# Merging the two halves of float64 weights: the low word's bits made on ScalarE, one VectorE pass instead of two

## The chip, the cores and the metric

The kernel runs on one core of one Trainium2 chip. The core has five engines that work side by side and wait for each other through semaphores: TensorE (PE; its weight loads are listed as PEld), VectorE (DVE), ScalarE (ACT), GpSimd (POOL) and SyncE (SP), which here mostly issues transfers. The metric is the time of one execution on the device, in microseconds (us); the time of a kernel is the median of several runs.

## The reference

The computation is a recurrent attention (an mLSTM) over 768 steps, for 4 batches and 8 heads of width 40, followed by a feed-forward layer over 3072 tokens of width 320 with 2048 hidden units:

```
for t in range(S):
    m_new = max(f[t] + m, i[t]);  f_s = exp(f[t] + m - m_new);  i_s = exp(i[t] - m_new)
    C = f_s * C + i_s * outer(v[t], k[t]);   n = f_s * n + i_s * k[t]
    y[t] = sigmoid(o[t]) * (C @ q[t]) / max(abs(n @ q[t]), 1)
h = x @ w_in                       # x: y by token, (3072, 320) @ (320, 2048)
g = max(h, 0) + alpha * min(h, 0)
out = g @ w_out                    # (3072, 2048) @ (2048, 320)
```

The weights w_in and w_out arrive as float64. The kernel computes in float32, with each operand of the large products split into a high part (fp32r) and a low part (the rest).

## The kernel before, in words

**Attention.** The recurrence is computed in chunks of 128 tokens, 24 chunks in all, two of which make a group of 256 tokens. For a chunk, TensorE makes scores from k and q by channel (tiles kf and qf), ScalarE makes the decays E as exponentials (L909 in the first group, L425 behind it), GpSimd masks them, VectorE weighs the scores (L933, L447), and TensorE multiplies them with the values and adds the part of the carried state C. The gated result xn is transposed, split (XH, XL, X2, X2L) and handed to the feed-forward layer.

**Feed-forward.** For each group there are eight steps fp. `up` makes 256 hidden units of 256 tokens (L593 to L600, in PSUM tile ph). ScalarE's Relu (L602) and a VectorE pass (L606) apply the slopes; a ScalarE cast makes the high part gh (L614) and VectorE or GpSimd the low part gl (L615). `down` multiplies them with the high and low parts of w_out (OH, OL) into po (L623).

**Weights.** Class `Weights` converts one tile. There are 18 tiles: eight of w_in with 128x512 values (t_wi), two that hold the rest of w_in's rows (t_wr, 128x512), and eight of w_out with 128x640 values (t_wo). A tile's raw float64 values are seen as pairs of 32-bit words: `raw[..., 1]` is the high word and `raw[..., 0]` the low word, so each is read at every second word. The steps are

1. `scale` (L696), on ScalarE: the high word, read as a float, goes through Prelu with a scale and a slope chosen so that the exponent is brought to float32's range and the sign is kept, in tile t.
2. `join` (L708 and L710), on VectorE: the bits of t are shifted left by 3, and then the top three bits of the low word (shifted right by 29) are merged in.
3. `high` (L718), on ScalarE: the cast to the high part WH, OH or W2.
4. `low` (L722), on VectorE: t less the high part.

The raw tiles of w_in lie in room that later holds parts of w_out; those of w_out share two buffers, so SyncE's queue loads a further one only when the step `join` has read an earlier one (L762).

**Order.** The work of the first group is written out by hand in the string ORDER: every name is a step (`w0s` is the scale step of weight tile 0, `w1h` its high part for tile 1, `kc1` and `qc1` copies of k and q by channel, `L1` a scan on VectorE, `wg10` a weighing, `warm12` twelve dummy matmuls that keep TensorE busy), and the instructions of each engine are chained in this order. ORDER covers the scale, join and split of tiles 0, 1 and 2. What follows it, from about 33 us on, is issued in the order of the program and placed on each engine by a planner, which goes by its own estimates of durations: the last tiles of the first half of w_in (`for t in w[3:]: t.all()`), then `convert("in", ...)` and `convert("out", ...)` ahead of the feed-forward steps that need them, interleaved with steps of the attention (`side`). All weights stay in SBUF from then on; the later groups convert none.

The functions around the change, with the line numbers of the profile:

Of the kernel before, what the change touches and what calls it, by code (L numbers as in the profile page):

```python
# [10 lines left out]
U32 = mybir.dt.uint32  # L11
BF16 = mybir.dt.bfloat16
AF = mybir.ActivationFunctionType
ALU = mybir.AluOpType
# [3 lines left out]
def kernel(ctx: ExitStack, tc: tile.TileContext, q, k, v, i_gate, f_gate, o_gate, w_in, w_out, alpha, out):  # L18
    nc = tc.nc
# [46 lines left out]
    def staging(name, tag):  # L66
        t = const.tile([P, NB * DM], U32, tag=tag, name=name)
        return t[:, : 2 * CW].rearrange("p (c w) -> p c w", w=2)

# [54 lines left out]
    def open_gate(b, c0=0, c1=NC):  # L124
        og = o_tiles[b][:, c0:c1]
        nc.scalar.activation(og, og, AF.Sigmoid)
# [14 lines left out]
    def weighed(n):  # L141

        b, c = divmod(n, NC)
        kd = sb.tile([P, H, D], F32, tag="kd", name=f"kd{n}")
        (nc.gpsimd if n in KDP else nc.vector).tensor_tensor(
            kd, by_token_of(n, 1), wT[:, c, b * H : (b + 1) * H].unsqueeze(2).broadcast_to([P, H, D]), ALU.mult
        )
        kds[n] = kd
# [152 lines left out]
    def values(n, E, busy=lambda: None):  # L301

        pH = psa(f"pH{n}")
        dense(pH, FILL.get(n, 0))
        va = va_t[n // GC % NV][:, n % GC]
        for i in range(H):
            if i % 2 == 0:
                busy()
            par, p = divmod(i, NPR)
            h = 2 * p + par  # L310
            nc.tensor.matmul(
                pH[:, h * VA : (h + 1) * VA], E[par][:, p * P : (p + 1) * P], va[:, h], start=True, stop=True
            )
        return pH[:, : H * VA].rearrange("p (h e) -> p h e", e=VA)
# [205 lines left out]
    def attention(n0):  # L520
# [45 lines left out]
    FILL = {3: 4, 4: 14, 5: 4}  # L566
    ORDER = """dq0 dq1 dw0 dw2 warm24 dv0 dw1 dw4 do1 dw3 do2 scan lf0a lf0b li0 lf0z L0 bj0 qT0 qc0 kT0 kc0 warm12 sp00
        bTt bTc l3a l3b alT l3c l3d warm6 wt0 ex00 sc00 l3e ms00 warm3 sp01 ewj ex01 ms01 sc01 warm3 eeL wg00 wTt eTt
        wTc eTc lf1a lf1b warm3 w0s wg01 sp10 alC ex10 ms10 warm3 sp11 ex11 qT1 w1s kT1 kc1 w0j0 warm4 li1 wd0 w0j1 w2s
        warm12 u0m qc1 u0c v0 w0h w0l w1j0 L1 w2j0 warm2 sc10 w1j1 warm2 w2j1 wd1 wg10 fsm fst sc11 ms11 warm6 dv1 dq3 wg11 og1  # L570
        lpa lpb bj1 dq2 dL dx2 w1h g0r dx0 g0g lpc lpd lpe g0x g0p w1l dx1 v1 x0 warm4 tadd g1r g1g s0a w2h g1x g1p w2l warm12 x1
        s1a s1d warm3 s0d og2"""

# [102 lines left out]
    class Weights:  # L676
# [11 lines left out]
        def scale(self):  # L688
            shape = list(self.raw.shape[:-1])
            t = late_pool.tile([P, 2 * DM], F32, tag="t", name=f"t_{self.name}", bufs=3)  # L690
            if len(shape) == 3:
                self.t = t.rearrange("p (f c) -> p f c", c=shape[2])
            else:
                self.t = t[: shape[0], : shape[1]]
            if self.double:
                nc.scalar.activation(  # L696
                    self.t, self.raw[..., 1].bitcast(F32), AF.Prelu, scale=2.0**-112, alpha=-(2.0**32)
                )
            else:
                for rows, src, _, _ in self.pieces:  # L700
                    nc.sync.dma_start(self.t[rows], src)

        def join(self, steps=range(2)):
            if self.double:
                t, lo = self.t.bitcast(U32), self.raw[..., 0]
                for step in steps:
                    if step == 0:
                        nc.vector.tensor_scalar(t, t, 3, None, ALU.logical_shift_left)  # L708
                    else:
                        nc.vector.scalar_tensor_tensor(t, lo, 29, t, ALU.logical_shift_right, ALU.bitwise_or)  # L710

        def parts(self, piece):
            rows, _, h, l = self.pieces[piece]
# [19 lines left out]

    ROOM = [["OH1", "OL1", "OH2"], ["OL2", "OH3"], ["OL3", "OH2", "OL2"], ["OH3", "OL3"]]
    CW = 512

    def load_w_in(i, kt):

        c0 = i * CW
        half, h0 = divmod(c0, DH)  # L740

        def part(X):
            return lambda: X[half][:, kt, h0 : h0 + CW]

        src = w_in[kt * P : (kt + 1) * P, c0 : c0 + CW]
        return Weights(f"wi{i}_{kt}", staging(f"wi{i}_{kt}", ROOM[i][kt]), [(slice(0, P), src, part(WH), part(WL))])

    def load_w_rest(i):

        pieces = []  # L750
        for e in range(2):
            cs = slice((i + e) * CW, (i + e + 1) * CW)
            rows, other = (slice(x * KR, (x + 1) * KR) for x in (e, 1 - e))
# [57 lines left out]
    def first_group():  # L811
# [12 lines left out]
        f, i, rst, m = fi[:, 0, :S], fi[:, 1, :S], rm[:, 0, :S], rm[:, 1, : S + 1]  # L824
# [4 lines left out]
        w = [None] * 5  # L829
# [115 lines left out]
        def warm(n=1):  # L945
            dense(junk, n)
# [19 lines left out]
        steps = {}  # L966
# [8 lines left out]
        def first_lf(j, t, engine):  # L975
            engine.tensor_tensor(lf[j], f[:, t], m[:, t], ALU.add)

        def second_lf(j, u, engine):
            engine.tensor_tensor(lf[j], lf[j], m[:, u], ALU.subtract)
# [37 lines left out]
        def later_decays():  # L1017
# [21 lines left out]
            lf1a=lambda: first_lf(1, t1, nc.gpsimd), lf1b=lambda: second_lf(1, u1, nc.gpsimd),  # L1039
            li0=lambda: nc.gpsimd.tensor_tensor(li[:, t0], i[:, t0], m[:, u0], ALU.subtract),  # L1040
            li1=lambda: nc.gpsimd.tensor_tensor(li[:, t1], i[:, t1], m[:, u1], ALU.subtract),
# [6 lines left out]
            wd0=lambda: weighed(0), wd1=lambda: weighed(1),  # L1048
            v0=lambda: got.update(h0=values(0, [E[0, 0], E[0, 1]], lambda: warm(V0))),
            v1=lambda: got.update(h1=values(1, [E[1, 0], E[1, 1]], lambda: warm(V1))),  # L1050
            og1=lambda: open_gate(0, 0, GC), og2=lambda: open_gate(0, GC, NC),
# [32 lines left out]
        for j in range(3):  # L1084
            steps[f"w{j}s"] = lambda j=j: w[j].scale()
            steps[f"w{j}h"] = lambda j=j: w[j].high()
            steps[f"w{j}l"] = lambda j=j: w[j].low()
            for step in range(2):
                steps[f"w{j}j{step}"] = lambda j=j, step=step: w[j].join([step])
        for name in ORDER.split():  # L1090
            if name.startswith("warm"):
                warm(int(name[4:]))
# [29 lines left out]
    late_pool = ctx.enter_context(tc.tile_pool(name="late", bufs=2))  # L1122
    start = len(nc.cur_bb.bb.instructions)
    first = first_group()
    next(first)
    pinned = pin(start)
# [81 lines left out]
```

## Time and profile before

| | |
|---|---|
| median of 3 runs | 497.78 us (497.69 to 501.44) |
| span of the profiled execution | 497.0 us (its time as a run is not given apart from this) |
| TensorE busy | 479.6 us, 97% of the span |
| VectorE busy | 324.1 us, 65% |
| ScalarE busy | 321.4 us, 65% |
| GpSimd busy | 305.9 us, 62% |
| conversion of the weight tiles | from 14.5 us (first Prelu) to about 98 us (last low part) |

The profile is one execution on the chip. Its page gives busy times of the engines; further views give the instructions of a line or a tile, what an engine waited for, the chain of work that ended last, the engines' instructions in order of time, and busy times by stretch of the span. In a list in order of time, a row has the start and the duration in us, then engine, line, operation and tiles, and in brackets the idle time before it and what ended that. A matmul's neighbours overlap, so rows of TensorE add up to more than the time they take together; the same holds in part for two instructions in a row on VectorE or ScalarE.

### The profile page before, as it was taken

The numbers are of one execution on the slowest core, as the hardware profiler recorded it, in microseconds if no ns is written. First come the engines' busy times: TensorE is split into PE (matmuls) and PEld (weight loads), VectorE is DVE, ScalarE is ACT, GpSimd is POOL, SyncE is SP. The second block draws the span as 40 slices with busy tenths as digits, with TensorE's granted clock in tenths as the row PEclk, the third lists the DMA queues.
The fourth block names the chain that finished last, engine by engine and source line by source line (L and its number), as shares of the span: only waits on it lengthen the run. The fifth ranks groups of instructions, "written<-read, shape, count | busy, mean of one in ns | idle before, by whom it ended". The sixth has DMA issues, their size and how long they took to land.

```text
span 497.0 us, 11890 instructions
## 1 busy us (share of the span) xinstructions
PE 479.6 (97%) x4509; PEld 458.3 (92%) x4509; DVE 324.1 (65%) x676; ACT 321.4 (65%) x700; POOL 305.9 (62%) x393
## 2 busy tenths in 40 slices
PE   8998889999999999999999999999999999999997
PEld 7877879899998999999899999989999999999997
DVE  7889899945668675675495576666586675642321
ACT  3869498555687776776975677677886663343332
POOL 6542163405559989849498789758888855243242
PEclk9999998999999999999999999999999999999999
DMA  9998977354685577587566675667664230000000
GB/s 171 232 167 235 248 192 216 94 94 96 150 183 118 125 171 160 105 191 151 111 148 131 147 134 123 157 166 139 134 171 76 46 90 1 1 28 1 26 1 26
DMA packets 173922, 61.60 MB, mean 124 GB/s; under 512 B 140154, under 2 KB 166122, under 8 KB 173866
## 3 DMA queue, kind: packets, MB, share of 16 engines
q1 hardware_dynamic: 173786, 60.75, 54.9%
q8 instruction: 35, 0.57, 0.5%
q14 instruction: 21, 0.17, 0.1%
q10 hardware_dynamic: 80, 0.11, 0.1%
HBM read 36.90 MB, written 4.03 MB: 82 GB/s over the span
## 4 chain that ended last, share of the span: by engine, by line
PE 64%; DVE 10%; ACT 8%; POOL 6%; DMA 5%; issue 5%; SPq 1%; ACTq 0%; DVEq 0%; POOLq 0%
PE po L623 25%; PE ph L593 4%; PE ph L596 3%; PE ph L594 3%; PE ph L597 3%; PE ph L599 3%; PE ph L595 3%; PE ph L600 3%; PE ph L598 3%; PE pH L347 2%; PE pS L441 2%; POOL gl L615 2%; PE warm L137 2%; DMA kS<-Z 2%; DMA qS<-Z 1%
## 5 line engine op out<-in xcount | busy, mean ns | idle before, releaser
L615 POOL TENSOR_TENSOR gl<-g,gh 128x512 fp32r<-128x512 f32 x80 | 102.8, 1286 | 62.0 <-ACT gh L614 54.7
L606 DVE SCALAR_TENSOR_TENSOR g<-g,oma,ph 128x256 f32<-128x256 f32 x160 | 69.8, 477 | 74.4 <-ACT g L602 68.8
L623 PE MATMUL po<-OH,gh 128*128 128x320 f32 x368 | 111.1, 314 | 0.6 <-ACT gh L614 0.6
L623 PE MATMUL po<-OL,gh 128*128 128x320 f32 x368 | 109.4, 310 | 0.0
L602 ACT ACTIVATE g<-ph 128x512 f32<-128x512 f32 x96 | 57.1, 595 | 41.0 <-PE ph L600 29.1
L614 ACT CAST gh<-g 128x512 fp32r<-128x512 f32 x80 | 49.5, 619 | 34.4 <-DVE g L606 33.0
L623 PE MATMUL po<-OH,gl 128*128 128x320 f32 x368 | 71.1, 315 | 0.2 <-POOL gl L615 0.2
L623 PEld LDWEIGHTS po<-OH,gh 128*128 128x128 f32 x368 | 69.0, 188 | 1.0 <-ACT gh L614 0.8
L623 PEld LDWEIGHTS po<-OL,gh 128*128 128x128 f32 x368 | 69.0, 188 | 0.0
L593 PE MATMUL ph<-XH,WH 128*128 128x256 f32 x192 | 58.1, 303 | 1.8 <-DVE g L606 0.8
L623 PEld LDWEIGHTS po<-OH,gl 128*128 128x128 f32 x368 | 56.8, 188 | 0.4 <-POOL gl L615 0.4
L425 ACT ACTIVATE E<-Lb,bT 128x128 f32<-128x128 f32 x160 | 51.0, 393 | 7.2 <-PE pH L347 7.1
L429 POOL TENSOR_SCALAR_AFFINE_SELECT E<-E 128x512 f32<-128x512 f32 x44 | 29.8, 677 | 40.7 <-ACT E L425 37.7
L597 PE MATMUL ph<-X,W 128*128 128x256 f32 x192 | 54.5, 285 | 0.0
L594 PE MATMUL ph<-XH,WH 128*128 128x256 f32 x192 | 54.3, 283 | 0.0
L596 PE MATMUL ph<-XH,WL 128*128 128x256 f32 x192 | 54.1, 282 | 0.0
L600 PE MATMUL ph<-X2L,W 128*128 128x256 f32 x192 | 54.0, 282 | 0.0
L599 PE MATMUL ph<-XL,WH 128*128 128x256 f32 x192 | 53.9, 281 | 0.0
L595 PE MATMUL ph<-XH,WL 128*128 128x256 f32 x192 | 53.7, 280 | 0.0
L598 PE MATMUL ph<-XL,WH 128*128 128x256 f32 x192 | 53.5, 279 | 0.0
L334 ACT CAST E<-pS 128x512 bf16<-128x512 f32 x72 | 41.8, 585 | 12.8 <-DVE pS L332 9.0
L593 PEld LDWEIGHTS ph<-XH,WH 128*128 128x128 f32 x192 | 36.2, 188 | 2.9 <-issue 1.0
(199 smaller groups left out, 1154.6 us busy)
## 6 DMA issues: line engine op xcount, KB each, us to landing
Lb<-L_d SPq DMA_DIRECT2D x20, 512.0 KB
wo<-in_moe_w_out_dram SPq DMA_DIRECT2D x8, 640.0 KB
wi<-in_moe_w_in_dram SPq DMA_DIRECT2D x8, 512.0 KB
qn<-in_q_dram SPq DMA_DIRECT2D x24, 160.0 KB
kn<-in_k_dram SPq DMA_DIRECT2D x24, 160.0 KB
va<-in_v_dram SPq DMA_DIRECT2D x24, 160.0 KB
og<-in_o_gate_dram SPq DMA_DIRECT2D x24, 160.0 KB
out_dram<-ob SPq DMA_DIRECT2D x11, 320.0 KB
```

What stands on the lines that cost most here:

```text
L593: nc.tensor.matmul(dst, WH[half][:, 0, hs], XH[:, 0], start=True, stop=False)
L594: nc.tensor.matmul(dst, WH[half][:, 1, hs], XH[:, 1], start=False, stop=False)
L595: nc.tensor.matmul(dst, WL[half][:, 0, hs], XH[:, 0], start=False, stop=False)
L596: nc.tensor.matmul(dst, WL[half][:, 1, hs], XH[:, 1], start=False, stop=False)
L597: nc.tensor.matmul(dst, W2[:, fs], X2, start=False, stop=False)
L598: nc.tensor.matmul(dst, WH[half][:, 0, hs], XL[:, 0], start=False, stop=False)
L599: nc.tensor.matmul(dst, WH[half][:, 1, hs], XL[:, 1], start=False, stop=False)
L600: nc.tensor.matmul(dst, W2[:, fs], X2L, start=False, stop=True)
L602: nc.scalar.activation(gt, ph, AF.Relu, scale=-1.0)
L606: nc.vector.scalar_tensor_tensor(out=y[:, e], in0=gt[:, e], scalar=oma[:, f : f + 1], in1=ph[:, e], op0=ALU.mult, op1=ALU.add)
L615: (nc.vector if g < 2 else nc.gpsimd).tensor_tensor(gl, y, gh.bitcast(F32), ALU.subtract)
L623: nc.tensor.matmul(po[j], x[:, e, j * P : (j + 1) * P], W[f // NB][:, f % NB], **ends)
```

## The change

The three bits of the low word are now made by ScalarE, as a number: the step `scale` gets a second instruction, which reads the low word as an unsigned integer, multiplies it by (just under) 2^-29, adds an offset near -0.5 and writes the rounded result, a number from 0 to 7, over the low word. The step `join` becomes one VectorE instruction, which shifts t left by 3 and merges that number in. In ORDER the two join steps of each tile become one, at the place of the second for tiles 0, 1 and 2.

```diff
-        wTc eTc lf1a lf1b warm3 w0s wg01 sp10 alC ex10 ms10 warm3 sp11 ex11 qT1 w1s kT1 kc1 w0j0 warm4 li1 wd0 w0j1 w2s
-        warm12 u0m qc1 u0c v0 w0h w0l w1j0 L1 w2j0 warm2 sc10 w1j1 warm2 w2j1 wd1 wg10 fsm fst sc11 ms11 warm6 dv1 dq3 wg11 og1
+        wTc eTc lf1a lf1b warm3 w0s wg01 sp10 alC ex10 ms10 warm3 sp11 ex11 qT1 w1s kT1 kc1 warm4 li1 wd0 w0j w2s
+        warm12 u0m qc1 u0c v0 w0h w0l L1 warm2 sc10 w1j warm2 w2j wd1 wg10 fsm fst sc11 ms11 warm6 dv1 dq3 wg11 og1
...
                 nc.scalar.activation(
                     self.t, self.raw[..., 1].bitcast(F32), AF.Prelu, scale=2.0**-112, alpha=-(2.0**32)
                 )
+                lo = self.raw[..., 0]
+                nc.scalar.activation(lo, lo, AF.Copy, scale=2.0**-29 * (1 - DL), bias=7.5 * DL - 0.5)
...
-        def join(self, steps=range(2)):
+        def join(self):
             if self.double:
-                t, lo = self.t.bitcast(U32), self.raw[..., 0]
-                for step in steps:
-                    if step == 0:
-                        nc.vector.tensor_scalar(t, t, 3, None, ALU.logical_shift_left)
-                    else:
-                        nc.vector.scalar_tensor_tensor(t, lo, 29, t, ALU.logical_shift_right, ALU.bitwise_or)
+                t = self.t.bitcast(U32)
+                nc.vector.scalar_tensor_tensor(t, t, 3, self.raw[..., 0], ALU.logical_shift_left, ALU.bitwise_or)
...
+    DL = 2.0**-9
...
-            for step in range(2):
-                steps[f"w{j}j{step}"] = lambda j=j, step=step: w[j].join([step])
+            steps[f"w{j}j"] = lambda j=j: w[j].join()
```

## The prediction

> **What bounds the kernel now.** I read the page first, for the busy shares, then a table of five stretches, because the page's averages mix a start-up in which weights are converted with a long steady part.
>
> ```profile
> span 497.0 us, 11890 instructions
> PE 479.6 (97%) x4509; PEld 458.3 (92%) x4509; DVE 324.1 (65%) x676; ACT 321.4 (65%) x700; POOL 305.9 (62%) x393
> core 0: us, PE busy (x) PEld busy (x) DVE busy (x) ACT busy (x) POOL busy (x), PEclk, DMA share, GB/s
> 14.00:33.00 19.00, 17.78 (x168) 15.45 (x166) 17.01 (x33) 12.75 (x30) 12.35 (x13) 1.00 1.09 210
> 33.00:50.00 17.00, 14.57 (x154) 12.85 (x154) 15.16 (x35) 16.38 (x33) 3.44 (x4) 1.00 0.76 209
> 50.00:58.00 8.00, 8.00 (x69) 7.80 (x66) 7.44 (x16) 1.80 (x4) 0.92 (x1) 1.00 1.02 274
> 58.00:77.00 19.00, 15.30 (x130) 13.23 (x129) 17.00 (x31) 18.59 (x44) 9.37 (x12) 0.95 0.79 212
> 77.00:98.00 21.00, 20.38 (x166) 19.74 (x166) 20.46 (x39) 15.08 (x34) 7.98 (x9) 0.97 0.47 138
> 98.00:497.00 399.00, 391.01 (x3751) 378.89 (x3749) 237.04 (x508) 251.78 (x546) 263.99 (x329) 1.00 0.49 106
> ```
>
> TensorE is the bound: from 98 us to the end it is busy 391.0 of 399. All 18 weight tiles are converted before 98 us, so the change can only move the moment at which TensorE reaches its steady load. What there is to win is TensorE's idle time in two stretches, 17 - 14.57 = 2.4 us (33 to 50) and 19 - 15.30 = 3.7 us (58 to 77), and a dip of its clock (below). In both stretches VectorE and ScalarE are nearly full together: ScalarE has 0.6 and 0.4 us free, VectorE 1.8 and 2.0. From 50 to 58 ScalarE does 1.8 us of work in 8 while TensorE is full, and from 77 to 98 it has 5.9 us free while TensorE is full again.
>
> **The change part by part.** The rows of the conversion, by line (durations are minimum/median/maximum in ns):
>
> ```profile
> L696 ACT ACTIVATE t_wi<-wi x8: 653/668/725, 14.5 to 79.7; 128x512 f32<-128x512 f32 x8
> L696 ACT ACTIVATE t_wo<-wo x8: 788/804/830, 43.2 to 89.6; 128x640 f32<-128x640 f32 x8
> L708 DVE TENSOR_SCALAR t_wi<-t_wi x8: 419/424/857, 15.9 to 81.3; 128x512 uint32<-128x512 uint32 x8
> L708 DVE TENSOR_SCALAR t_wo<-t_wo x8: 437/493/1099, 44.2 to 91.2; 128x640 uint32<-128x640 uint32 x8
> L710 DVE SCALAR_TENSOR_TENSOR t_wi<-wi,t_wi x8: 673/692/1205, 19.5 to 82.9; 128x512 uint32<-128x512 uint32 x8
> 33.67 1.23 ACT t_wi L696 x2
> 69.78 1.51 ACT L696 ACTIVATE t_wo<-wo 128x640 f32<-128x640 f32 x2
> 58.00:77.00 19.00, 3.29 (x6) 0.95 0.79 212
> ```
>
> Removed: the shift L708, 18 times. The last row above is that line alone from 58 to 77 us: 3.29 us, of which the slowest took 1.10. Kept: the merge L710, one pass over the same two operands with their roles exchanged, so I cost it as unchanged. Added: 18 ScalarE copies of the low words, read and written as integers at every second word. Two Prelu passes back to back take 1.23 us where one takes 0.67, so one more costs ScalarE 0.56; for 640 columns 1.51 - 0.80 = 0.71. Ten tiles have 512 columns and eight 640: 10 x 0.56 + 8 x 0.71 = 11.3 us more on ScalarE. No row shows ScalarE reading or writing integers. Lower bound 0.56, since the copy handles as many words as Prelu; upper bound one merge pass of VectorE over the same strided words, 0.69. I take 0.56, the pass of the same engine over the same tile; the upper end would add 18 x 0.13 = 2.3 us of ScalarE time.
>
> The Trainium skill ("ScalarE: Activation LUTs", section "What ACT_TABLE_LOAD costs") gives 186 ns + 0.833 ns per element with immediate scale and bias, and an overlap of about 93 ns back to back; by it the copies would be an estimated 10.2 us instead of 11.3. No run here shows the copy itself. The same page's "Rules for kernel authors" would keep a multiply and add on VectorE, which speaks against this change; the rows agree as to one pass (424 ns on VectorE, 668 on ScalarE), but they also show a VectorE pass of up to 1.10.
>
> First stretch, 14 to 33 us, where the order is written by hand and can be followed:
>
> ```profile
> 15.93 2.17 ACT L909 ACTIVATE E<-pb,bT 128x128 f32<-128x128 f32 x8 [0.77 <-PE pb L898]
> 17.94 0.72 ACT L696 ACTIVATE t_wi<-wi 128x512 f32<-128x512 f32 x1
> 19.71 0.68 ACT L696 ACTIVATE t_wr<-wr 128x512 f32<-128x512 f32 x1
> 21.56 0.69 DVE L722 TENSOR_TENSOR WL<-t_wi,WH 128x512 fp32r<-128x512 f32 x1 [0.24 <-ACT WH L718]
> 22.17 0.42 DVE L708 TENSOR_SCALAR t_wi<-t_wi 128x512 uint32<-128x512 uint32 x1
> 22.50 1.21 DVE L982 TENSOR_TENSOR_SCAN g_L<-g_WL,g_lf 32x512 f32<-32x512 f32 x1
> 25.26 0.69 DVE L933 TENSOR_TENSOR E<-pS,E 128x512 f32<-128x512 f32 x1
> ```
>
> The copy behind the first tile's Prelu is hidden by the 0.77 us that ScalarE waits for TensorE. The other two (behind 17.94 and 19.71) push the k and q copies and then the cast WH by 1.1 us. VectorE waits for that cast until 21.56, so it too is 1.1 later; behind it stand the scan L982, the merges and the weighing L933, for which the scores and all of x wait. Two shifts ahead of L933 go; the first holds VectorE from 22.17 to 22.50, and I take the second alike: 2 x 0.33 = 0.7. The first tile's shift goes too, but its room is lost again in the wait for ScalarE. L933 and all behind it: 1.12 - 0.66, **+0.5 us**. The dummy matmuls fill the wait and hide nothing of it.
>
> Second stretch, 33 to 50. From here a planner orders each engine, and I assume that it keeps the order shown.
>
> ```profile
> 38.10 0.49 ACT g L602
> 38.61 0.49 DVE ph L606
> 44.17 0.49 DVE L708 TENSOR_SCALAR t_wo<-t_wo 128x640 uint32<-128x640 uint32 x1
> 47.21 0.39 PE L593 MATMUL ph<-XH,WH 128*128 128x256 f32 x1 [0.71 <-DVE gl L615]
> ```
>
> The chain runs on ScalarE from the two Prelu at 33.67 to the first Relu at 38.10 and then on VectorE. Two copies behind those Prelu delay the Relu by 2 x 0.56 = **+1.1**; an output tile's copy at 43.2 delays the casts behind it, gh among them, by **+0.7**; the shift at 44.17 goes, **-0.4**. At 47.2 TensorE is 0.5 + 1.1 + 0.7 - 0.4 = 1.9 us late, and stays so through 50 to 58, where it is full.
>
> Third stretch, 58 to 77.
>
> ```profile
> 58.05 0.79 ACT L696 ACTIVATE t_wo<-wo 128x640 f32<-128x640 f32 x1 [2.42 <-DMA wo<-in_moe_w_out_dram]
> 59.89 0.56 ACT L284 COPY qf<-pq 104x512 f32<-104x512 f32 x1
> 60.49 0.38 PE L419 MATMUL pb<-LP,pick 96*128 96x128 bf16 x4 [1.01 <-ACT qf L284]
> 60.61 0.42 DVE t_wi L708
> 68.53 0.41 DVE t_wr L708
> 72.72 1.10 DVE L708 TENSOR_SCALAR t_wo<-t_wo 128x640 uint32<-128x640 uint32 x1
> SPq L762 <- DVE t_wo L710: 5.5, 3, 2.6
> ```
>
> ScalarE waits there for an output weight until 58.05; its lateness is taken up by that wait of 2.42 us as far as the transfer itself isn't late. SyncE's queue issues that load once the merge L710 has read an earlier raw tile (last row); the merge moves with VectorE, so I put the landing +0.5 late (bounds 0 and 1.9). Behind the Prelu stand two more, and now three copies, 0.71 + 2 x 0.56 = 1.8, before qf, for which TensorE waits. So at 60.5 TensorE is 0.5 + 1.8 = 2.3 late; the 1.9 brought along is inside this, since TensorE already waited 1.01. From 60.6 to 74.5 the chain is mostly VectorE's and loses four shifts: 0.42, 0.41, 1.10 and one more of an output tile at its least, 0.44, together **-2.3** without their overlaps. Against it three copies (one wr, two wo, 0.56 + 1.4) lie between the exponentials that the masks and weighings wait for; I charge half, **+1.0**. Each merge now waits for a copy and not just for Prelu: +0.56 to 0.71 less the shift of 0.42 to 0.49, +0.2 each, and VectorE has other work queued. At 77: 2.3 - 2.3 + 1.0 = **+1.0 us**. From 77 to 98 TensorE is full and VectorE's gain changes nothing; ScalarE's five copies fall into its 5.9 us of room.
>
> The profiled span is 497.0; the median of the runs shown is 497.78, so 0.8 lies around it, and the profile gives no other time of that execution. 497.0 + 1.0 + 0.8 = **498.8 us**.
>
> **Rivals.** *VectorE alone is the bound* of both full stretches. Then the third stretch gives its 3.3 us of shifts back, and the second some 1.2 of TensorE's 2.4. The clock speaks for more:
>
> ```profile
> 72.00:74.00 2.00, 0.85 (x6) 0.49 (x5) 2.00 (x4) 1.95 (x5) 1.85 (x2) 1.00 0.62 92
> 74.00:76.00 2.00, 1.52 (x10) 1.19 (x10) 1.97 (x3) 1.94 (x4) 1.76 (x3) 0.75 0.76 211
> 76.00:78.00 2.00, 2.00 (x12) 1.75 (x11) 1.94 (x4) 1.47 (x3) 0.00 (x0) 0.50 1.11 360
> 78.00:80.00 2.00, 2.00 (x18) 2.00 (x18) 1.88 (x4) 1.42 (x5) 0.00 (x0) 0.90 0.91 323
> 58.00:62.00 4.00, 2.33 (x22) 1.98 (x21) 3.04 (x8) 3.96 (x10) 0.44 (x1) 1.00 0.87 217
> ```
>
> Behind two microseconds in which TensorE worked 0.85, the granted clock fell to 0.75, 0.50 and 0.90: 0.5 + 1.0 + 0.2 = 1.7 us lost. With the first stretch's 0.5 and without that hole: 497.8 + 0.5 - 1.2 - 3.3 - 1.7 = 492.1. Against it: ScalarE is fuller than VectorE in both stretches.
>
> *ScalarE becomes the bound, and a second clock dip follows* (slower). Second stretch: four copies, 2 x 0.56 + 2 x 0.71 = 2.5, into 0.6 of room: +1.9. Third: six, 3 x 0.56 + 3 x 0.71 = 3.8, into 0.4: +3.4. With the 0.5 that is +5.8, 503.6. If qf at 60 us comes over 1.8 late, TensorE's 2.33 busy of 4 become 2.33 of 6, the share of 72 to 74, and the clock could fall there too: +1.7, 505.3. It decides where the copies stand ahead of the casts and exponentials. For it: 18.59 of 19. Against: the 6.2 us ScalarE has free just before.
> The Trainium skill ("TensorE: Matmul & The Clock Gate", "Part 1: The HAM clock gate") halves the clock after an idle window of about 3.4 us; the 0.50 row agrees with the half, though TensorE was never idle that long by these rows.
>
> *The exchange doesn't take place as costed*: the integer copy at its upper bound adds 2.3 us to ScalarE, of which the six copies of the third stretch, 0.8, would show: 499.6, inside the forecast's case. *The planner writes another order* behind 33 us: TensorE's 8 us idle after 98 can grow or shrink by a few; 494 to 502.
>
> **How the numbers follow.** A measurement here tells about 1%, 5 us, from no change. Forecast (net within about 3 us, 495.8 to 501.8) 0.55; VectorE bound 0.15, some two thirds of it below 492.8; ScalarE bound 0.18, most of it above 502.8; another order 0.12, a quarter of it beyond 1% on either side. Faster 0.10 + 0.03 = 0.13; slower 0.14 + 0.03 = 0.17; same 0.70. The range leaves out a tenth at each end: 493.0, near the VectorE case, to 504.0, past the ScalarE case without the dip.
>
> **What would show it.** No TENSOR_SCALAR on the weights and 18 more ACTIVATE at 0.56 to 0.71 apart; L933 near 25.8 instead of 25.26; the first Relu near 39.7; ScalarE over 18.9 of 19 in the third stretch; qf near 62; the dip of the clock still there. The prediction is wrong if TensorE's idle time from 58 to 77 shrinks by more than 2 us or grows by more than 3, if the dip is gone or doubled, or if a copy takes over 0.9 us.

## The result and the profile after

| | before | changed |
|---|---|---|
| median | 497.85 us (496.04 to 501.44, 20 runs) | 501.57 us (500.25 to 504.78, 20 runs) |
| ratio | | 1.0078, 95% interval 1.0062 to 1.0094 |
| span of the profiled execution | 497.0 us | 499.7 us |

The change makes the kernel 3.7 us slower, 0.8%. The forecast was 498.8, in a range of 493.0 to 504.0: the time lies in the range and within 1% of before, but the sum of the steps, +1.0, came out 2.7 too low. One execution, of the first run of `tied` below, took 918.6 us; it is left out of the median and the ratio given there.

The page of the changed kernel, and the same stretches as before (columns: engine's busy us and instructions, then the granted clock, the share of the DMA engines, GB/s):

```profile
span 499.7 us, 11876 instructions
PE 480.6 (96%) x4509; PEld 459.8 (92%) x4509; DVE 312.8 (63%) x658; ACT 331.8 (66%) x718; POOL 304.5 (61%) x393
14.00:33.00 19.00, 17.64 (x164) 15.01 (x162) 13.24 (x27) 13.16 (x30) 11.66 (x13) 1.00 1.11 212
33.00:50.00 17.00, 13.18 (x107) 11.30 (x108) 10.96 (x28) 16.03 (x28) 2.10 (x3) 0.76 0.68 199
50.00:58.00 8.00, 8.00 (x73) 7.49 (x71) 5.72 (x11) 6.37 (x16) 2.61 (x3) 0.86 1.09 258
58.00:77.00 19.00, 17.54 (x159) 16.80 (x159) 15.50 (x34) 17.75 (x41) 4.84 (x8) 1.00 0.75 198
77.00:98.00 21.00, 19.44 (x173) 18.51 (x172) 19.02 (x33) 20.10 (x44) 8.96 (x11) 1.00 0.54 141
98.00:499.00 401.00, 392.98 (x3760) 380.88 (x3758) 238.31 (x512) 253.15 (x551) 266.43 (x332) 1.00 0.49 107
```

VectorE has 18 instructions and 11.3 us less, ScalarE 18 more and 10.4 us more: the exchange took place. From 98 us to the end of the span TensorE is idle for 8.7 us (401.7 - 392.98; 8.0 before, 399 - 391.01), and it has 2.0 us more work left. So 2.0 of the 2.7 us between the spans are lost before 98, in the stretch where the weights are converted. There TensorE's idle time grew from 33 to 50 (2.4 to 3.8) and from 77 to 98 (0.6 to 1.6), and shrank from 58 to 77 (3.7 to 1.5); from 14 to 98 it adds up to nearly the same, 8.2 us against 8.0. What differs is the granted clock: mean 0.76 from 33 to 50 and 0.86 from 50 to 58, where it was 1.00. That is 0.24 x 17 + 0.14 x 8 = 5.2 us, against 1.6 before (0.95 of 19 and 0.97 of 21). So in this execution the clock takes 3.6 us more, which is of the size of the loss; where the time went is read from this, and not why the clock fell. Over whole executions, the median of the mean clocks is 0.989 against 0.999 (the latter from the 49 executions of the kernel before that stand beside the experiments), so at most 1.0% of 500 us, 5 us, of TensorE's time goes to the clock that way (less where TensorE would have waited anyhow).

The new instructions, by line (minimum/median/maximum in ns), the merge, and ScalarE's instructions in order of time around 36 us:

```profile
L700 ACT ACTIVATE wi<-wi x8: 651/686/717, 15.0 to 73.2; 128x512 uint32<-128x512 uint32 x8
L700 ACT ACTIVATE wo<-wo x8: 758/797/835, 47.1 to 90.2; 128x640 uint32<-128x640 uint32 x8
L708 DVE SCALAR_TENSOR_TENSOR t_wi<-t_wi,wi x8: 639/688/1662, 16.5 to 82.5; 128x512 uint32<-128x512 uint32 x8
35.99 0.67 ACT L696 ACTIVATE t_wi<-wi 128x512 f32<-128x512 f32 x1
36.54 0.69 ACT L700 ACTIVATE wi<-wi 128x512 uint32<-128x512 uint32 x1
37.10 0.70 ACT L696 ACTIVATE t_wi<-wi 128x512 f32<-128x512 f32 x1
```

A copy costs ScalarE 0.56 (from its start at 36.54 to the next Prelu at 37.10), as predicted, and the merge with its operands exchanged costs what it cost (688 against 692 ns).

What was not predicted stands between 31 and 42 us, ScalarE and TensorE of the changed kernel first, then ScalarE of before:

```profile
33.85 0.65 ACT L700 ACTIVATE wi<-wi 128x512 uint32<-128x512 uint32 x1 [3.04 <-DMA wi<-in_moe_w_in_dram]
34.41 0.35 ACT L488 CAST XH<-p 128x256 fp32r<-128x256 f32 x1
34.81 0.38 PE L593 MATMUL ph<-XH,WH 128*128 128x256 f32 x1 [1.50 <-ACT XH L488]
42.04 0.57 ACT L602 ACTIVATE g<-ph 128x512 f32<-128x512 f32 x1
```

```profile
31.69 0.37 ACT L488 CAST XH<-p 128x256 fp32r<-128x256 f32 x1 [1.21 <-PE p L469]
38.01 0.57 ACT L602 ACTIVATE g<-ph 128x512 f32<-128x512 f32 x1
```

The planner has put one copy of a w_in tile ahead of the second cast XH, although it belongs behind a Prelu that comes later. ScalarE stands in that copy for 3.04 us until the tile has landed; the cast is 2.7 us later than before, and the first Relu comes at 42.04 instead of the 39.7 that I gave it (a further copy, at 40.96, also stands ahead of it). So the order behind 33 us, which I had assumed to stay, did not.

### The profile page after: what moved, and what is told of

It reads as the page before. It is cut to its first block, busy times and chain, and to the rows that moved or that the text cites. A ratio compares the mean times of both kernels' runs of the same rounds, so it can differ in the third digit from the quotient of the medians.

```text
span 499.7 us, 11876 instructions
## 1 busy us (share of the span) xinstructions
PE 480.6 (96%) x4509; PEld 459.8 (92%) x4509; DVE 312.8 (63%) x658; ACT 331.8 (66%) x718; POOL 304.5 (61%) x393
## 4 chain that ended last, share of the span: by engine, by line
PE 60%; ACT 11%; DMA 8%; SPq 7%; DVE 7%; issue 5%; POOL 2%; ACTq 0%; POOLq 0%; DVEq 0%
PE po L623 26%; PE ph L593 4%; PE ph L596 3%; PE ph L597 3%; PE ph L594 3%; PE ph L599 3%; PE ph L600 3%; PE ph L598 3%; PE ph L595 3%; PE pS L441 3%; PE pH L347 3%; SPq L122 3%; ACT E L425 2%; SPq L686 2%; DMA kS<-Z 2%
## 5 line engine op out<-in xcount | busy, mean ns | idle before, releaser
L623 PE MATMUL po<-OH,gh 128*128 128x320 f32 x368 | 111.4, 314 | 0.0
L623 PE MATMUL po<-OL,gh 128*128 128x320 f32 x368 | 109.7, 310 | 0.0
L614 ACT CAST gh<-g 128x512 fp32r<-128x512 f32 x80 | 49.5, 619 | 34.8 <-DVE g L606 32.5
L623 PE MATMUL po<-OH,gl 128*128 128x320 f32 x368 | 71.3, 315 | 0.2 <-POOL gl L615 0.2
L623 PEld LDWEIGHTS po<-OH,gh 128*128 128x128 f32 x368 | 69.1, 188 | 0.2
L623 PEld LDWEIGHTS po<-OL,gh 128*128 128x128 f32 x368 | 69.2, 188 | 0.0
L623 PEld LDWEIGHTS po<-OH,gl 128*128 128x128 f32 x368 | 56.8, 188 | 0.4 <-POOL gl L615 0.4
```

What stands on the lines that cost most here:

```text
L623: nc.tensor.matmul(po[j], x[:, e, j * P : (j + 1) * P], W[f // NB][:, f % NB], **ends)
```

## The experiments

These are the theories, by the letters that the expectations give them. H: the loss is this one copy that waits. L: it is ScalarE's load, the copies' time wherever they stand. C: it is the clock, 1.7 us for each further piece at half. O: it is the order that the planner makes of the changed work, as a whole. H and L stood at first; Q and its rival E came with the last but one kernel shown here. Each kernel below was timed in five rounds against the kernel before on the same chip.

### The copy tied to its Prelu, one copy free, the copy alone, no shift

`tied` holds each copy behind the Prelu of its own tile on ScalarE's queue; `free_one` does this for all tiles but the one whose copy stood at 33.85.

```diff
+ first = nc.cur_bb.bb.instructions[-1]          # the Prelu
  nc.scalar.activation(lo, lo, AF.Copy, ...)
+ tc.add_manual_dep(nc.cur_bb.bb.instructions[-1], first.name, ..., reason="order")   # free_one: if self.name != "wi2_0"
```

> The change, with each copy of the low words held behind the Prelu of its own tile on ScalarE. Theory H (one early copy): in the changed kernel the planner put the copy of a w_in tile of the third column block ahead of the x casts of the first group, where ScalarE then stood 3.04 us for that tile's transfer; this delay and the dips of the granted clock behind it are the loss, and the rest is near the prediction's sum of +1.0. It expects 498.0 to 499.5 us, the second XH cast at 32.0 to 32.3 us instead of 34.41, and no clock under 0.9 from 34 to 54. Rival L (ScalarE's load): the 18 copies themselves cost the time wherever they stand; it expects 501 to 502.5, and ScalarE over 95% busy from 33 to 50 and 58 to 77 with TensorE waiting for its casts.

> As the run before, but the copy of one tile alone (third column block of w_in, first 128 rows) is left free, and so stands ahead of the second XH cast again. Theory H expects the loss back: 500.5 to 502 us, XH near 34.4, the clock under 0.8 somewhere from 34 to 50. A rival within H, that the other early copies (four or more of them stand ahead of Relu, gh or k/q copies in the changed kernel) make much of the loss, expects 499 to 500. Rival L expects the time of the run before, within 0.5 us.

`tied` took 502.87 us, ratio 1.0114 (1.0078 to 1.0149); `free_one` 501.88, 1.0082 (1.0059 to 1.0106). In `free_one` the hole is back: ScalarE stands in the copy for 2.48 us, and the cast XH comes at 33.92. Run again for its profile, beside other kernels, `tied` gave 502.30, 1.0116 (1.0088 to 1.0144):

> The copies held behind their Prelu, once more, for its profile: theory H (one early copy makes the loss) has fallen with 502.96 us, and the question is what does. Theory L (ScalarE is the late one): 501.5 to 503 us, the second XH cast near 32.3 us, and ScalarE over 95% busy from 33 to 50 and from 58 to 77 with TensorE's waits on its casts. Theory C (the clock): the loss is that of more windows at half clock, 1.7 us each; at the same mean clock as the kernel before the time is the same.

ScalarE in order of time, of this second run:

```profile
31.58 0.37 ACT L488 CAST XH<-p 128x256 fp32r<-128x256 f32 x1 [1.21 <-PE p L469]
39.04 0.57 ACT L602 ACTIVATE g<-ph 128x512 f32<-128x512 f32 x1
```

The cast is back at its old place and the first Relu comes 1.0 us late, not 4.0; the kernel isn't faster for it, nor slower in `free_one` with the hole. H, which gave `tied` 498.0 to 499.5, has fallen: the hole of 3 us is real, but it is not the loss. L still stood: in this profile ScalarE is busy 16.23 us of 17 from 33 to 50 and 18.89 of 19 from 58 to 77.

`copy_only` is `tied` with both passes of VectorE kept; `no_shift` leaves out the copy and the shift and merges the low bits with the unshifted high part, so the weights have other values and the work is less than the reference needs.

```diff
+ nc.vector.tensor_scalar(t, t, 3, None, ALU.logical_shift_left)                                     # copy_only
+ nc.vector.scalar_tensor_tensor(t, lo, 0, t, ALU.logical_shift_right, ALU.bitwise_or)               # copy_only
+ nc.vector.scalar_tensor_tensor(t, lo, 29, t, ALU.logical_shift_right, ALU.bitwise_or)              # no_shift: this alone
```

> The copies held behind their Prelu, and the two VectorE passes kept (shift, then a merge with a shift of zero): ScalarE's added work alone, nothing saved. By the prediction's sum VectorE's shifts are worth 0.7 in the first stretch, 0.4 in the second and 2.3 in the third, so 498.8 + 3.4 = 502 us. If VectorE's passes are covered, the time is that of the tied kernel within 1 us. Rival L expects 501 to 503 here and in the tied kernel alike.

> The two passes without the shift, and no copy (the merge with the unshifted high part is the one of the kernel before; the weights' values are therefore other ones): VectorE's saving alone. By the prediction's sum 0.7 + 0.4 + 2.3 less: 494.5 us. If VectorE is the bound of both full stretches and the clock's hole at 74 goes too: 491.5 to 493. If VectorE's passes are covered: 497 to 498.

`copy_only` took 504.16, 1.0131 (1.0107 to 1.0155); `no_shift` 497.02, 0.9981 (0.9958 to 1.0003). So taking VectorE's 18 shifts away, with nothing put in their place, is worth 0.9 us by the medians (497.89 before), and its interval reaches no change; with the copies there it is 1.3 us (504.16 - 502.87). The sum of the prediction had 3.4 for them. The copies cost about 6 (504.16 - 497.89 = 6.3; 502.87 - 497.02 = 5.9). `no_shift` too has an order of its own from the planner. Where its gain goes, two windows and two rows of TensorE show:

```profile
58.00:77.00 19.00, 17.14 (x150) 15.49 (x149) 16.39 (x28) 18.85 (x47) 6.39 (x10) 1.00 0.88 236
77.00:98.00 21.00, 19.14 (x163) 18.48 (x163) 17.90 (x36) 14.76 (x34) 8.23 (x11) 1.00 0.54 126
85.37 0.60 PE L137 MATMUL pH<-ident 128*128 128x256 bf16 x4 [1.20 <-DVE E L447]
105.28 0.42 PE L623 MATMUL po<-OH,gh 128*128 128x320 f32 x1 [1.39 <-ACT gh L614]
```

From 58 to 77 TensorE does gain 1.8 us (17.14 busy for 15.30), but 1.2 of it are given back from 77 to 98 (19.14 for 20.38), where it now waits 1.20 us for a weighing on VectorE, and 0.5 from 98 to 125 (25.61 for 26.07 of 27), where it waits 1.39 us for a cast gh. From 58 to 77 VectorE is rid of the shifts, 3.3 us of work before, and ScalarE is as full as before, 18.85 of 19; that it was ScalarE that kept the rest of the 3.3 from TensorE is argued from this and not shown. The clock takes a part too: 0.993 is the median of its runs, 3.5 us at most, where the kernel before had 0.997 beside it.

### A part of the tiles at a time

`first7`, `mid6` and `last5` take the new way, tied, for the first seven tiles, the six of 58 to 77 us, and the last five; the others keep two passes.

```diff
+ if self.name in ONE_PASS:   # first7 / mid6: wo4 wi2_0 wi2_1 wr2 wo6 wo8 / last5: wi3_0 wi3_1 wo10 wo12 wo14
      nc.vector.scalar_tensor_tensor(t, t, 3, lo, ALU.logical_shift_left, ALU.bitwise_or)
+     return
+ ...                         # the two passes of before
```

> Only the first seven tiles in the new way (tiles 0 to 2 of the written order, the next two of w_in, the first two of w_out), the other eleven by two VectorE passes. Theory L: the second stretch has 0.6 us of ScalarE's time for 2.5 us of copies and the first stretch passes its lateness on, so +1.5 to +3 us here: 499.4 to 501. Theory C: +1.7 per further window of half clock and none otherwise. If the loss is all later: 497 to 498.5.

> Only the six tiles of the third stretch in the new way (three of w_in's third block and its rest, three of w_out). Theory L: 3.8 us of copies into 0.4 us of ScalarE's room, less what VectorE's shifts are worth there: +1 to +3 us, 499 to 501. By the prediction's sum for this stretch (copies +1.8 and +1.0, shifts -2.3): +0.5, 498.4. If VectorE is the bound there: -1 to -3.

> Only the last five tiles in the new way, where ScalarE has 5.9 us of room and VectorE is over 97% busy. Prediction and theory L: no change, 497.3 to 498.3 us, or up to 1 us faster where VectorE's relief lets the gate's load start earlier. Against both: slower by over 1 us, if ScalarE's order matters more than its free time.

They took 501.25, 501.21 and 500.95 us: 1.0080 (1.0060 to 1.0100), 1.0088 (1.0068 to 1.0109), 1.0088 (1.0056 to 1.0120). Each part alone costs about 4 us, as much as the whole. So the loss isn't a price per copy, and L in its plain form has fallen too: seven, six or five copies cost what eighteen do, and L gave `last5` no loss at all.

The parts don't lose it in one way. The median of the mean clocks is 0.987 for `first7`, so that the clock could cover its loss; for `mid6` it is 0.996, some 2 us at most, and the rest is waiting, so C alone doesn't explain it. `last5` lies between (0.995), and its runs reach from 497.5 to 504.7. Its profiled execution was the fastest of them, 497.5 at 0.999 and so level with before, and shows the exchange of one hole for another:

```profile
58.00:77.00 19.00, 16.51 (x150) 15.02 (x149) 17.90 (x33) 18.62 (x45) 9.97 (x12) 1.00 0.83 216
98.00:125.00 27.00, 24.26 (x187) 23.99 (x187) 11.04 (x22) 14.79 (x26) 7.63 (x13) 1.00 0.42 88
106.84 0.41 PE L623 MATMUL po<-OH,gh 128*128 128x320 f32 x1 [2.74 <-ACT gh L614]
```

From 58 to 77 TensorE gains 1.2 us; from 98 to 125 it is idle for 2.7 (0.9 before), all of it in one wait for a cast gh. Another order has other holes, and the other five runs, at 0.990 to 0.997, lose some clock besides.

### Work and order exchanged

This leaves O, and it can be tested by separating work from order. `new_in_old_order` has the changed work, with the instructions of every engine and of SyncE's queue in the order of the kernel before, each copy directly behind its Prelu. `old_in_new_order` has the work of before in the order of the changed kernel, each shift directly ahead of its merge. The chains hold within one engine only, so they add no wait between engines.

```diff
+ORDERS = ["3 4 5 6 ...", ...]            # per engine: the other kernel's order, as numbers of instructions
+for text in ORDERS:
+    for k in text.split():               # each instruction behind the one ahead of it
+        tc.add_manual_dep(ins[int(k)], last.name, ..., reason="order")
```

> The change's work in the order of the kernel before: on every engine and in SyncE's queue all instructions stand in the order of the kernel before, the shifts are gone, and each copy stands directly behind its Prelu. This is the case that the prediction's sum was made for. Theory O (order: what the planner made of the changed program is the loss, and any of the part changes so far cost the same 4 us because each got another order): near the prediction's sum, 497.5 to 499.5 us. Theory L (the copies on ScalarE are the loss): 500.5 to 502.5 us, with ScalarE late at TensorE's waits in the second and third stretch.

> The reverse: the work of the kernel before (shift and merge on VectorE, no copy) with every instruction in the order that the changed kernel has, each shift directly ahead of its merge. Theory O: the loss is there without the copies, 500.5 to 502 us. Theory L: no loss without the copies, 497 to 498.5 us. If both play a part, 499 to 500.5.

| | order of before | order of the changed kernel |
|---|---|---|
| work of before | 497.13 us | 503.10 us, 1.0116 (1.0096 to 1.0135) |
| changed work | 507.27 us, 1.0181 (1.0146 to 1.0216) | 501.57 us, 1.0078 (1.0062 to 1.0094) |

(The last entry is from the rounds of the result, where the kernel before took 497.85.) Both kernels took longer than any theory gave: O had 497.5 to 499.5 and 500.5 to 502, L 500.5 to 502.5 and 497 to 498.5. Neither work nor order alone is the loss. Each work is fastest in the order made for it. In the order of before the change costs 9 to 10 us (by the ratio and by the medians), in the planner's new order 3.7, some 6 less. That order isn't merely worse: the old work loses 6 us in it, with two waits for a weighed decay matrix E that before doesn't have at this length. Its median clock is 0.986, so part of the 6 can be the clock's. Waits of `old_in_new_order` (us in all, times, longest):

```profile
PE pS L476 <- DVE E L478: 2.4, 1, 2.4
PE pH L342 <- DVE E L963: 2.1, 1, 2.1
```

`new_in_old_order` is also the kernel on which my sum can be checked row by row, since it meets the assumption of the prediction. Its lines are 31 further down (the scale step L696 is L727 here, gh L614 is L645, po L623 is L654). TensorE's instruction that stood at 60.49 now stands at 62.66, that is +2.2 where I had +2.3; the ones for xn at 73.53 and 78.10 stand at 74.34 and 77.74, 0.8 late and 0.4 early, where I had +1.0 at 77. Ten microseconds later the sum breaks. ScalarE and TensorE in order of time, and the windows, of `new_in_old_order`, and then TensorE and ScalarE of the kernel before:

```profile
62.66 0.39 PE L450 MATMUL pb<-LP,pick 96*128 96x128 bf16 x4
74.34 0.44 PE L500 MATMUL p<-ident,xn 128*128 128x128 f32 x2 [0.36 <-POOL xn L432]
77.74 0.31 PE L500 MATMUL p<-ident,xn 128*128 128x128 f32 x1
90.08 0.79 ACT L731 ACTIVATE wo<-wo 128x640 uint32<-128x640 uint32 x1
90.75 0.58 ACT L645 CAST gh<-ph 128x512 fp32r<-128x512 f32 x1
93.52 0.80 ACT L727 ACTIVATE t_wo<-wo 128x640 f32<-128x640 f32 x1 [2.18 <-DMA wo<-in_moe_w_out_dram]
91.39 0.63 PE L654 MATMUL po<-OH,gh 128*128 128x320 f32 x1 [4.47 <-ACT gh L645]
58.00:77.00 19.00, 17.18 (x156) 15.80 (x155) 14.52 (x29) 18.94 (x46) 6.95 (x11) 1.00 0.66 166
77.00:87.00 10.00, 9.92 (x84) 9.72 (x82) 7.39 (x13) 9.92 (x22) 2.73 (x4) 1.00 0.61 189
87.00:91.40 4.40, 0.01 (x1) 0.01 (x1) 3.97 (x8) 4.34 (x8) 2.51 (x3) 0.94 0.60 185
91.40:98.00 6.60, 6.60 (x30) 6.41 (x30) 4.94 (x8) 2.80 (x6) 1.60 (x2) 0.50 0.15 59
98.00:104.50 6.50, 6.50 (x30) 6.50 (x31) 3.67 (x8) 4.27 (x11) 2.83 (x4) 0.50 0.43 99
```

```profile
73.53 0.44 PE L469 MATMUL p<-ident,xn 128*128 128x128 f32 x2 [1.11 <-POOL xn L401]
78.10 0.44 PE L469 MATMUL p<-ident,xn 128*128 128x128 f32 x1
87.37 0.59 ACT L614 CAST gh<-ph 128x512 fp32r<-128x512 f32 x1 [0.44 <-DVE ph L606]
89.62 0.81 ACT L696 ACTIVATE t_wo<-wo 128x640 f32<-128x640 f32 x1 [1.66 <-DMA wo<-in_moe_w_out_dram]
```

ScalarE is busy 18.94 of 19, then 9.92 of 10 and 4.34 of 4.40: it never catches up. The cast gh comes at 90.75 instead of 87.37, 3.4 late, directly behind a copy. TensorE, which was on time at 77.74, has nothing to do for 4.47 us, and then finds its clock at half until 104.5 (30 matmuls in 6.60 us). The matmul that stood at 96.59 before stands at 105.83, 9.2 us late, and that is most of the 10.4 us between the spans (507.4 and 497.0). Of the six executions this one took longest, 509.15 us at a clock of 0.976: two others took 503.16 and 503.78 at 0.990 and 0.989, so some 6 us are lost without the full length of this half clock, and 4 more with it. The copies were priced rightly; their lateness was carried past the stretch in which they stand.

### The six copies of the third stretch taken out

If the queue of ScalarE from 58 to 91 us is the cause (Q), the six tiles of 58 to 77 must carry most of it, though they stand 10 us and more ahead of the hole. `no_mid_copies` is `new_in_old_order` with two VectorE passes for these six.

```diff
+TWO = "wo4 wi2_0 wi2_1 wr2 wo6 wo8".split()
+if self.name not in TWO:
     nc.scalar.activation(lo, lo, AF.Copy, ...)
```

> The change's work in the order of the kernel before, as in new_in_old_order, but the six tiles of the third stretch (58 to 77 us) keep their two VectorE passes and have no copy. With all 18 copies in that order ScalarE ran from 58.2 to 91.3 us without a gap, its cast gh came at 90.75 instead of 87.37, and TensorE stood 4.47 us for it, behind which its clock was at half for 13.65 us. Theory Q (ScalarE's queue: the six copies of the third stretch, carried along a queue without gaps, are what TensorE waits for at 88): 2.5 us of copies remain against 2.3 us of gaps, so gh is under 1 us late, the long half clock behind it is gone, and the time is 498 to 501 us. Rival E (the early part: the seven copies before 50 us and the half clock from 39.7 to 50 are what costs): 503 to 506 us, with TensorE still about 2 us late at 60 and the wait at 88 no shorter than 3 us.

It took 501.50 us, 1.0078 (1.0053 to 1.0104): 5.8 us less by the medians, for six copies of 0.56 to 0.7 each, but only about 2 less than the two executions of `new_in_old_order` at 503. Its ScalarE and TensorE in order of time (lines 33 further down than before) and windows:

```profile
87.89 0.58 ACT L647 CAST gh<-ph 128x512 fp32r<-128x512 f32 x1
88.53 0.41 PE L656 MATMUL po<-OH,gh 128*128 128x320 f32 x1 [2.70 <-ACT gh L647]
33.00:50.00 17.00, 15.04 (x142) 13.21 (x141) 13.07 (x31) 16.68 (x31) 3.27 (x4) 0.90 0.73 181
77.00:98.00 21.00, 18.30 (x137) 17.92 (x137) 16.95 (x32) 16.67 (x38) 6.42 (x8) 0.92 0.47 136
```

The cast is 0.5 late instead of 3.4, the wait 2.70 instead of 4.47, and the half clock lasts 3.4 us instead of 13.65. Q holds for the larger part. Not for all: the time is a little above what was expected, and TensorE still waits at 88, because the matmuls ahead of it ended 1.6 us sooner (85.83 for 87.39): the kernel before loses 1.7 us there to its dip of the clock from 75 us on, which this kernel doesn't have (1.00 from 58 to 77). By these rows the dip before took time in which TensorE would else have waited for this cast. Against the profile of before, the clock loses 1.7 us more from 33 to 50 (0.90 of 17) and as much from 77 to 98 (0.92 of 21), less the 0.95 of 19 and 0.97 of 21 there, 1.6: about 2 us of the 2.8 between the spans (499.8 and 497.0).

### The bits on GpSimd

A version that could beat both would take the bits off ScalarE and VectorE alike. `pool_bits` has GpSimd make them, which before has 62% of work.

```diff
- nc.scalar.activation(lo, lo, AF.Copy, scale=2.0**-29 * (1 - DL), bias=7.5 * DL - 0.5)
+ nc.gpsimd.tensor_scalar(lo, lo, 2.0**-29 * (1 - DL), 7.5 * DL - 0.5, ALU.mult, ALU.add)
```

> The low word's bits made by GpSimd instead of ScalarE, with the same multiply and add, each placed behind the GpSimd instruction that the program issues before it; VectorE has the one pass. GpSimd is busy 3.4 of 17 us and 9.4 of 19 in the two stretches. Theory L: ScalarE is relieved of the copies, so the time is that of VectorE's saving alone, 496 to 498 us. Theory O: it has an order of its own again, 500 to 502 us, whatever engine makes the bits.

It took 508.05, 1.0205 (1.0171 to 1.0240), above both expectations. Its line, and what GpSimd waited for ahead of it:

```profile
L701 POOL TENSOR_SCALAR wo<-wo x8: 760/944/2229, 64.3 to 106.4; 128x640 uint32<-128x640 uint32 x8
DMA wo<-in_moe_w_out_dram: 11.0, 3
```

GpSimd's queue stood 11.0 us waiting for output weights, and what stood behind in its queue stood with it; the conversion lasts until 106 us. GpSimd's room is in its average only. No version beat the kernel before: `no_shift`, which came out level, isn't the whole computation.

## Why the prediction was right or wrong

**TensorE as the bound, and only what lies before 98 us counts**: right but for 0.7 us. TensorE is idle for 8.7 us behind 98 against 8.0, and has 2.0 us of work left over from before it.

**The prices.** Copies 0.56 (measured 0.56), the merge unchanged (688 against 692 ns), L933 at 25.8:

```profile
25.57 0.69 DVE L932 TENSOR_TENSOR E<-pS,E 128x512 f32<-128x512 f32 x1
```

+0.3 for +0.5 (in `new_in_old_order` it stands at 25.11, 0.15 early). All right; the rival that the exchange isn't as costed is out.

**Second stretch**, +1.9 at 47: in the order that I assumed (`new_in_old_order`), TensorE was 3.4 late there. The two copies behind the two Prelu show first in a wait for g_WH, an exponential of the gates that ScalarE makes ahead of the Relu; before and in `new_in_old_order`:

```profile
37.53 0.43 PE L864 MATMUL ps_ge<-ident,g_WH 32*128 32x32 f32 x4 [0.60 <-ACT g_WH L1106]
38.51 0.43 PE L895 MATMUL ps_ge<-ident,g_WH 32*128 32x32 f32 x4 [1.71 <-ACT g_WH L1136]
```

That is the +1.1 that I gave the Relu, 1.71 - 0.60. The rest is not in my sum: from 39.7 us on the clock stood at half for 10.24 us, while TensorE had work almost without a break. The size of that isn't given by the wait, since `no_mid_copies` has the same wait of 1.71 us and 3.41 us at half behind it. In the changed kernel the stretch lost 1.4 us of TensorE's time to idling and about 4 to the clock (0.76 of 17). I had foreseen a clock dip only in the third stretch and only in a rival. Term mis-sized: no clock in it.

**Third stretch**, +2.3 at 60.5 and +1.0 at 77: in the assumed order +2.2, then +0.8 at 73.5 and -0.4 at 78. The numbers are near, but in part by luck. The price of the copies ahead of qf was right: qf stands at 61.76 instead of 59.89, +1.9. But TensorE didn't wait for qf. It was busy 4.00 of 4 us from 58 to 62 (2.33 before), with the 3.3 us that it brought along, of which the wait of 1.01 us took up a part; I had the 1.9 brought along vanish in that wait. By 73.5 it was down by 1.4, where shifts and copies together had -2.3 + 1.0 = -1.3. At 78 TensorE is early only because the dip of the clock from 75 on isn't there, which I had expected to stay.

**"From 77 to 98 ... ScalarE's five copies fall into its 5.9 us of room"**: this step failed. The room was an average of a stretch. At its start ScalarE was 3 to 4 us behind from the full stretch, and TensorE reached the next cast gh before that was made up: 3.4 us for the late cast, then the clock at half for 13.65 us in the execution shown. The 5.9 us of room lay mostly behind this cast; before, ScalarE waits 1.66 us for a transfer right after it, and in `new_in_old_order` 2.18. In the changed kernel's own order the two stretches change roles: ScalarE is busy 17.75 of 19 from 58 to 77, under the 18.9 that I gave as a sign, and 20.10 of 21 from 77 to 98.

**"I assume that it keeps the order shown"**: failed, and in the other direction than I had feared. The new order cost one hole of 3 us and gave back some 6. So the forecast was close partly because two errors cancel: in the order assumed, +1.0 should have been +9 to +10, and that order wasn't kept.

**0.8 us around the span**: mis-sized. All later executions, which have a time and a span each, lie 1.66 to 1.83 us over their span, so the execution profiled of before took about 498.7 and was not a median one. That moves no difference, as both kernels carry it.

**The rivals.** *VectorE the bound* is out: without its shifts and without copies the kernel gains 0.9 us, not the 5.7 that this rival gave (497.8 - 492.1). *ScalarE the bound, with a second clock dip* (503.6 to 505.3) is the nearest in kind: in the assumed order it is what took place, and larger, with the dips at 39.7 and 90.9 us and not at 60. *Another order* took place too, and 501.57 is within its 494 to 502. Of the marks that I set for being wrong, two came true although the time lay in the range: the idle time from 58 to 77 shrank by 2.2 us, and the clock's dip moved and is three times as long (10.24 us at half against 3.41).

**What stays open.** That first, middle and last tiles cost 4 us each and don't add up fits "another order", but not every hole has been followed. About 1 us of `no_mid_copies` isn't placed. `mid6` loses about 4 us nearly without the clock, `first7` perhaps all by it, and no run takes the clock alone away. So it stays open how much of the changed kernel's 3.7 us is waiting and how much the clock behind it. The mean clock doesn't fix the time either: four executions of `no_mid_copies` at 0.986 took as long, 501.15 to 501.60 us, as one at 0.992, 501.48. That the copy came free to move ahead because it needs no buffer t, while its Prelu does, is read from the code and wasn't tried. And the cost of the planner's order can't be split further: no order was searched for by hand.

## What to carry to other kernels

When work is moved from an engine with some room to one that is full, don't credit room in a later stretch: the full engine's queue is late when it gets there, so look for the first instruction behind the full stretch that the bounding engine waits for, and ask whether room comes ahead of it. A hole of some microseconds in TensorE's work costs more than itself, since the clock may follow it; a sum without that term is too low. Where a planner sets the order, pin the old order and exchange work and order crosswise: only so is it seen what the work costs and what the order costs.

## What the runs showed of the hardware

The granted clock falls to half for whole pieces of 3.41 us: 3.41, 6.83, 10.24 and 13.65 us were seen in these traces, and 6.83 in the changed kernel:

```profile
33.00:35.00 2.00, 0.50 (x5) 0.39 (x6) 0.20 (x1) 1.15 (x4) 0.25 (x1) 1.00 0.63 250
35.00:38.50 3.50, 3.50 (x18) 3.50 (x18) 1.95 (x7) 3.47 (x6) 0.00 (x0) 0.52 0.01 2
45.40:52.20 6.80, 5.99 (x30) 5.06 (x30) 6.46 (x16) 6.78 (x15) 0.94 (x1) 0.50 1.00 241
```

Behind two microseconds in which TensorE was busy 0.5, it ran 3.4 us at half though busy throughout; the second time it was half for 6.83 us, behind 6.9 us with 1.5 of idling. The piece agrees with the Trainium skill ("TensorE: Matmul & The Clock Gate", section "What's actually happening"), which speaks of a free-running activity window of about 3.4 us. But TensorE was idle for no more than 1.50 us at a time ahead of 35.1 in the changed kernel: less than a whole window of idleness was enough. Nor does the length of a hole decide it: in the profiled execution of `last5` the wait of 2.74 us at 106.84 had no half clock behind it (1.00 from 98 to 125).

An integer copy in place at every second word costs ScalarE what a float pass does, 686 ns for 512 columns. GpSimd needs 944 ns where ScalarE needs 797, for 640.
